# Attention and a mixture of experts in one kernel: a second block of tokens chosen from six batches' counts

## The chip, the cores and the metric

The kernel runs on one core of one Trainium2 chip. The metric is the device time of one execution, in microseconds; of the kernel before there are three, 904.43, 906.6 and 909.86 us, with a median of 906.6. Engines: TensorE (PE in rows), VectorE (DVE), ScalarE (ACT), GpSimd (POOL), and SyncE (SP), which here only issues DMAs.

## The reference

Eight batches of 448 tokens, 12 heads of 64. Attention with a soft cap on the scores, then for each token the one expert of eight with the largest logit, a two-layer network, scaled by the probability of that expert:

```python
def _attn_ref(q, k, v, cap):                      # (8, 12, 448, 64)
    scores = np.matmul(q, k.transpose(0, 1, 3, 2)) / np.sqrt(64)
    scores = cap * np.tanh(scores / cap)
    attn = softmax(scores)
    return np.matmul(attn, v)
...
def _moe_ref(x, w_gate, w1, w2):                  # (3584, 768), (768, 8), (8, 768, 1024), (8, 1024, 768)
    logits = x @ w_gate
    expert_idx = np.argmax(logits, axis=1)
    gate_w = softmax(logits)[np.arange(N), expert_idx]
    for e in range(8):
        xe = x[expert_idx == e]
        out[expert_idx == e] = gate_w * (np.maximum(xe @ w1[e], 0.0) @ w2[e])
```

## The kernel before

**Attention** runs in 48 steps, one for each pair of heads (six to a batch), and the steps overlap by hand. In step n TensorE makes the scores of pair n (`scores`, two parts), ScalarE their tanh and exp, VectorE adds up the parts of the probabilities (`adds`, whose second half ends with an addition on GpSimd, line 285, up to step 45), and TensorE multiplies the probabilities of pair n - 1 with V (`pv`). A list of tasks (`at(step, when, ...)`, run by `do`) puts the other work between these parts: the sums of the probabilities and the logits of a batch on TensorE, then on VectorE, batch by batch, the reciprocals (`rec_v`, `rec_c`), the logits (`log_v`), the choice of an expert (`route_v`, `route_g`), the scaling (`scale`), and the place of each token in its expert's list (`place_v`). SyncE stores the finished rows to DRAM (`store`), GpSimd scatters the token numbers to a list in DRAM (`place_d`, four scatters a batch). `filler` holds generators of small VectorE instructions; each `fill()` in the code runs one of them.

**Loads of Q, K and V** come by SyncE for two pairs at a time (`load(g, part)`). Before, K is asked for at the start of each even step and Q and V at the start of the next; the buffers are those of two groups earlier, so the transfer waits for the scores that still read them, and what is behind it on SyncE's queue waits too.

**The experts** work on blocks of tokens of one expert: large ones of 448 and small ones of 256. In a block, `up(j, f)` makes the half chunk f of the hidden layer (18 matmuls) and `down(j, f)` adds its share to the output (18 more), f from 0 to 7. Weights and x are float32, split into a high part (a cast on ScalarE, `high`) and what is left of it (a subtraction on VectorE or, with `e=G`, on GpSimd, `low`); three products of such halves stand for one. So each chunk of weights costs a cast and a subtraction, and x costs, for each of six pieces, a transposition on VectorE (`trans_x`), a cast on ScalarE and a subtraction on VectorE (`split_x`). h is split likewise behind `up`: a relu on ScalarE and one instruction of VectorE.

Which tokens form a block is known from the counts of all eight batches, from which VectorE works out tables (`tables`, some 40 small instructions). One block, number -1, is chosen earlier, from the counts of the first four batches (`first_block`): the expert with most tokens, in groups of 56. Its weights are loaded by SyncE in 16 chunks (`load_w0`, 384 KB each), its x gathered by GpSimd in 14 pieces of 128 rows (`load_x`) during the last steps of attention. The other eight (`ORDER`: six large, two small) get weights and x by gathers of GpSimd with the tables' indices; weights are not loaded again where a block has the expert of the one before. If the tables find more blocks than these, a branch at the end runs them.

The stretch that the change touches most is written out by hand: steps 42 to 48, then block -1 (`up(-1, 0)` to `down(-1, 7)`), between whose chunks the last two batches are routed and the tables are made, and then the start of the next block. Instructions of an engine run in the order of this text.

Of the kernel before, what the change touches and what calls it, by code (L numbers as in the profile page):

```python
# [18 lines left out]
E = 8  # L19
# [11 lines left out]

LARGE = 448
SMALL = 256
GROUP = 56
B_FIRST = 4

NL = (T - B_FIRST * S // E + E * (LARGE - SMALL - 1)) // LARGE
NS = E

ORDER = [0, 1, 2, 3, 4, 5, NL, NL + 1]  # L40
# [84 lines left out]
def attention_moe(tc, qT, kT, vL, capd, wgL, w1a, w1b, w2a, w2b, cst, cmk, out):  # L125
# [6 lines left out]

    n_first = (B_FIRST + 1) * NP + 1

# [404 lines left out]
    f0 = {}  # L539
# [3 lines left out]
    def first_block():  # L543
        cnt = att.tile([128, E], F32, name="cnt0")
        V.tensor_tensor(out=cnt, in0=base, in1=cb0, op=ALU.subtract)
        mx = att.tile([128, 1], F32, name="mx0")
        V.tensor_reduce(out=mx, in_=cnt, axis=AX.X, op=ALU.max)

        th = att.tile([128, LARGE // GROUP], F32, name="th0")
# [3 lines left out]
        k = keep.tile([128, 3], F32, name="k56")  # L553
        V.tensor_reduce(out=k[:, 0:1], in_=th, axis=AX.X, op=ALU.add)
        for i, f in ((1, -float(GROUP)), (2, GROUP / LARGE)):
            V.tensor_scalar(out=k[:, i : i + 1], in0=k[:, 0:1], scalar1=f, scalar2=None, op0=ALU.mult)
        V.tensor_scalar(out=cnt, in0=cnt, scalar1=mx, scalar2=None, op0=ALU.subtract)
        em, oh = first_max(cnt, [128, E], keep, "fb")
        e0 = keep.tile([128, 1], F32, name="e0")
        V.tensor_scalar(out=e0, in0=em, scalar1=8.0, scalar2=None, op0=ALU.add)  # L560
        t = att.tile([128, 2], F32, name="t0")
        V.tensor_scalar(out=t[:, 0:1], in0=e0, scalar1=128.0, scalar2=pcol, op0=ALU.mult, op1=ALU.add)
        V.tensor_scalar(
            out=t[:, 1:2], in0=e0, scalar1=float(T // QB), scalar2=kcol(C_IN), op0=ALU.mult, op1=ALU.add
        )

# [3 lines left out]
        V.tensor_tensor(out=t[:, 1:2], in0=t[:, 1:2], in1=mx, op=ALU.add)  # L570
        ti = keep.tile([128, 2], I32, name="t0i")
        V.tensor_copy(out=ti, in_=t)
        row = nc.values_load(
            ti[0:1, 0:1],
# [5 lines left out]
        f0.update(e0=e0, oh=oh, ti=ti, row=row, less=k[:, 1:2], part=k[:, 2:3])  # L580
# [3 lines left out]
    def tables():  # L584

        def tl(shape, name, dt=F32):
# [8 lines left out]
        V.scalar_tensor_tensor(  # L595
            out=cnt, in0=f0["oh"], scalar=f0["less"], in1=cnt, op0=ALU.mult, op1=ALU.add
        )
        yield 1
# [34 lines left out]
        for i, s, w in parts:  # L633
# [44 lines left out]
        V.tensor_scalar(  # L678
            out=first, in0=ej, scalar1=f0["e0"], scalar2=f0["part"], op0=ALU.is_equal, op1=ALU.mult
        )  # L680
        yield 1
        V.tensor_tensor(out=pr, in0=pr, in1=first, op=ALU.add)
        yield 1
# [17 lines left out]
        V.tensor_copy(out=prev[:, 0:1], in_=f0["e0"])  # L701
# [69 lines left out]
    def load_w0(i):  # L771

        f, r, w = (i, w1r, w1L) if i < FC else (i - FC, w2r, w2L)
        c = f % 4 * DM
        nc.sync.dma_start(out=r[f // 4][:, f % 4, :], in_=w[f // 4][bass.ds(f0["row"], 128), c : c + DM])
# [32 lines left out]
    def load_ids(j):  # L808
# [5 lines left out]
        idx = f0["ti"][:, 1:2] if j < 0 else tab["lidx"][:, j : j + 1]  # L814
# [29 lines left out]
    def load_x(j, gs=None):  # L844
        xi = idt[j][0]
        rows = 4 * S * (B_FIRST if j < 0 else B)
        for g in gs or range(groups(j)):
            gather(xg[:, g, :], xd[0:rows, :], xi[:, g : g + 1], rows - 1)
# [26 lines left out]
    def up(j, f):  # L875
# [11 lines left out]
        hb = h0 if j < 0 and f < 3 else m["hb"]  # L887
# [4 lines left out]
    def down(j, f, cs=range(2)):  # L892
        hh, hl = hs[j, f]
        wh, wl = w2s[f]
        if f == 0 and cs[0] == 0:
            if j < 0:
# [29 lines left out]
    def evac(j, cs=range(2)):  # L926
        y = m["y"]
        if cs[0] == 0:
            ys[j] = ys0 if j < 0 else m["yo"].tile([128, QB * XW], F32, name="ys")
# [41 lines left out]
    for b in range(B):  # L971
# [20 lines left out]
        at(n + 5, 0, store, b, range(0, 2))  # L992
        at(n + 5, 1, place_v, b)
        at(n + 6, 0, store, b, range(2, 4))
# [4 lines left out]
    at(n_first, 1, first_block)  # L999
    for i in range(2 * FC):  # L1000
        at(n_first + 1 + i, 1, load_w0, i)

    at(n_first + 4, 1, load_ids, -1)
    at(n_first + 6, 1, make_idx, -1)

    g = 0
    for i in range(7):
# [346 lines left out]
```

## Time and profile before

| | us |
|---|---|
| median of three runs | 906.6 |
| the profiled execution | 905.34 |
| its span in the profile | 903.6 |
| TensorE busy, matmuls | 838.4 (93%) |
| VectorE busy | 548.7 (61%) |
| ScalarE busy | 483.9 (54%) |
| GpSimd busy | 466.0 (52%) |
| mean granted clock of TensorE | 0.977 |

Attention fills the first 380 us, the nine blocks of the experts the rest. The page names lines of the kernel: 248 and 260 are the scores, 249, 263, 266 and 268 tanh and exp, 277 and 285 the adds, 300 and 310 the product with V, 884 `up`, 908 and 916 `down`, 889 and 890 the split of h, 791 and 796 the split of weights, 858, 864 and 865 that of x, 750 the gathers, 527 the scatters of token numbers. A timeline row gives the start, the duration, the engine, the operation with the tiles that it writes and reads, how many instructions are merged into it, and in brackets how long the engine had been idle and what released it.

### The profile page before, as it was taken

The numbers are of one execution on the slowest core, as the hardware profiler recorded it, in microseconds if no ns is written. First come the engines' busy times: TensorE is split into PE (matmuls) and PEld (weight loads), VectorE is DVE, ScalarE is ACT, GpSimd is POOL, SyncE is SP. The second block draws the span as 40 slices with busy tenths as digits, with TensorE's granted clock in tenths as the row PEclk, the third lists the DMA queues.
The fourth block names the chain that finished last, engine by engine and source line by source line (L and its number), as shares of the span: only waits on it lengthen the run. The fifth ranks groups of instructions, "written<-read, shape, count | busy, mean of one in ns | idle before, by whom it ended". The sixth has DMA issues, their size and how long they took to land. (4 is left out here: it accounts for less than half of the span.)

```text
span 903.6 us, 12040 instructions
## 1 busy us (share of the span) xinstructions
PE 838.4 (93%) x4492; PEld 557.4 (62%) x4492; DVE 548.7 (61%) x885; ACT 483.9 (54%) x573; POOL 466.0 (52%) x382
## 2 busy tenths in 40 slices
PE   8999999999999996786999999999999999999893
PEld 3222322222223221265989989899999999999893
DVE  3559797979797965777373763744735537356520
ACT  7988889888978883632332532332423324234410
POOL 1423353434343645653718857577577575665600
PEclk9999999999999997998999999999999999999997
DMA  5231545454527572404455312453431124444100
GB/s 202 70 123 62 182 65 181 65 181 66 180 97 210 173 246 89 64 16 126 154 202 193 127 27 62 180 188 128 169 127 53 32 64 176 183 177 173 65 34 33
DMA packets 45155, 111.67 MB, mean 124 GB/s; under 512 B 8561, under 2 KB 27411, under 8 KB 42016
## 3 DMA queue, kind: packets, MB, share of 16 engines
q1 hardware_dynamic: 28384, 50.72, 19.6%
q0 software_dynamic: 16416, 59.87, 18.8%
q8 instruction: 37, 0.61, 0.3%
q14 instruction: 30, 0.25, 0.1%
q10 hardware_dynamic: 288, 0.23, 0.1%
HBM read 101.40 MB, written 22.36 MB: 137 GB/s over the span
## 5 line engine op out<-in xcount | busy, mean ns | idle before, releaser
L285 POOL TENSOR_TENSOR p<-p,pr 64x896 f32<-64x896 f32 x46 | 103.4, 2248 | 206.7 <-DVE p L277 150.3
L889 ACT ACTIVATE hb<-ph 128x448 fp32r<-128x448 f32 (+1 forms) x69 | 34.9, 508 | 296.7 <-PE ph L884 208.1
L890 DVE SCALAR_TENSOR_TENSOR hb<-ph,hb 128x448 fp32r<-128x448 f32 (+1 forms) x69 | 39.3, 574 | 202.6 <-ACT hb L889 202.5
L249 ACT ACTIVATE pt<-sp,qsc 128x896 f32<-128x896 f32 x144 | 138.7, 997 | 35.0 <-PE sp L248 34.9
L750 POOL DMA_INDIRECT xg<-xd,xi x114 | 134.5, 1180 | 37.9 <-issue 30.4
L248 PE MATMUL sp<-qr,kr 64*128 64x448 f32 x576 | 136.9, 580 | 11.1 <-ACT pt L249 10.9
L266 ACT ACTIVATE pt<-pt,capt 128x1792 f32<-128x1792 f32 (+1 forms) x96 | 134.9, 1406 | 2.3
L310 PE MATMUL po<-pt,vr 128*64 128x448 f32 x576 | 132.4, 568 | 0.0
L760 POOL DMA_INDIRECT out<-ys,xi x98 | 107.9, 1101 | 29.2 <-issue 27.0
L248 PEld LDWEIGHTS sp<-qr,kr 64*128 64x128 f32 x576 | 47.8, 187 | 98.7 <-ACT pt L249 43.7
L277 DVE TENSOR_TENSOR p<-pt 128x896 f32<-128x896 f32 x48 | 58.3, 1214 | 48.9 <-ACT pt L266 48.9
L310 PEld LDWEIGHTS po<-pt,vr 128*64 128x64 f32 x576 | 33.5, 138 | 76.4 <-issue 74.4
L277 DVE TENSOR_TENSOR p<-p,pt 128x896 f32<-128x896 f32 x48 | 53.8, 1121 | 9.6 <-ACT pt L266 9.5
L864 ACT CAST xh<-xt 128x448 fp32r<-128x448 f32 (+1 forms) x54 | 27.2, 532 | 42.6 <-DVE xt L858 42.6
L527 POOL DMA_INDIRECT ids<-tok,slots x32 | 38.4, 1200 | 10.9 <-issue 6.3
L319 DVE COPY ot<-po 128x448 f32<-128x448 f32 x48 | 29.7, 619 | 20.7 <-PE po L310 20.5
L300 PE MATMUL po<-pr,vr 64*64 64x448 f32 x192 | 25.0, 565 | 15.1 <-ACT pr L268 14.2
L750 POOL DMA_INDIRECT w1r<-in_w1b,widx x8 | 11.1, 1382 | 46.1 <-DVE w17l L796 45.5
L858 DVE STREAM_TRANSPOSE xt<-xg 128x448 f32<-128x448 f32 (+1 forms) x54 | 30.3, 585 | 7.3 <-DMA xg<-xd,xi 6.4
L865 DVE TENSOR_TENSOR xl<-xt,xh 128x448 fp32r<-128x448 f32 (+1 forms) x54 | 28.8, 559 | 2.6 <-ACT xh L864 2.5
L934 DVE STREAM_TRANSPOSE ys<-y 128x448 f32<-128x448 f32 x36 | 19.8, 612 | 12.8 <-DMA out<-ys,xi 7.3
L300 PEld LDWEIGHTS po<-pr,vr 64*64 64x64 f32 x192 | 5.3, 131 | 33.2 <-ACT pr L268 31.5
(410 smaller groups left out, 1970.6 us busy)
## 6 DMA issues: line engine op xcount, KB each, us to landing
vr<-in_vL SPq DMA_DIRECT2D x24, 448.0 KB, 6.2
kr<-in_kT SPq DMA_DIRECT2D x23, 448.0 KB, 3.7
qr<-in_qT SPq DMA_DIRECT2D x23, 448.0 KB, 6.0
xd<-yt SPq DMA_DIRECT2D x20, 336.0 KB, 6.8
xd<-w2r SPq DMA_DIRECT2D x12, 336.0 KB, 5.8
xg<-xd,xi POOLq DMA_INDIRECT x114, 3.1
out<-ys,xi POOLq DMA_INDIRECT x98, 2.4
w1r<-in_w1a SPq DMA_DIRECT2D x4, 384.0 KB, 6.2
```

Of the source, the lines that this page charges most:

```text
L248: PE.matmul(sp[:, j, 0:S], kr[r, i, c], qr[r, i, :], start=True, stop=True)
L249: A.activation(out=pt[:, 2 * g : 2 * g + 2, :], in_=sp[:, 0:2, 0:S], func=AF.Tanh, scale=qsc)
L266: A.activation(out=pt[:, lo:hi, :], in_=pt[:, lo:hi, :], func=AF.Exp, scale=capt)
L277: V.tensor_tensor(out=p4, in0=pt[:, 0:2] if half == 0 else p4, in1=pt[:, 2 * half + 2 : 2 * half + 4], op=ALU.add)
L285: e.tensor_tensor(out=p4[r], in0=p4[r], in1=rests[n // 2][r], op=ALU.add)
L300: PE.matmul(pvs[n + i][64 * j : 64 * j + 64, 0:S], vr[r, 12 + j, :], rests[n // 2][r, j], start=True, stop=False,)
L310: PE.matmul(po[64 * j : 64 * j + 64, 0:S], vr[:, n % 2 * 6 + 3 * j + t, :], pt[:, 2 * t + j], start=False, stop=t == 2,)
L527: i = G.indirect_dma_start(out=ids, out_offset=bass.IndirectOffsetOnAxis(ap=slots[0:p, c : c + 1].bitcast(U32), axis=0), in_=tok[0:p, c : ...
L750: G.indirect_dma_start(out=dst, out_offset=None, in_=src, in_offset=bass.IndirectOffsetOnAxis(ap=idx.bitcast(U32), axis=0), bounds_check=b ...
L760: i = G.indirect_dma_start(out=dst, out_offset=bass.IndirectOffsetOnAxis(ap=idx.bitcast(U32), axis=0), in_=src, in_offset=None, bounds_che ...
L889: A.activation(out=hh, in_=ph, func=AF.Relu)
L890: V.scalar_tensor_tensor(out=hl, in0=ph, scalar=0.0, in1=hh, op0=ALU.max, op1=ALU.subtract)
```

## The change

A second early block, number -2, is chosen by the same function from the counts of six batches, less what block -1 takes. `ORDER` has one large block fewer. Its choice is handed out as small instructions by `fill()` from the end of step 42 on, the rest of it at the end of step 46; its 14 gathers of x are issued in steps 47 and 48; its weights come by SyncE, each of 16 chunks right behind the split that frees its place (`split`). Everything of block -1 moves one to two steps ahead: its choice from step 31 to 30, its weight chunks from steps 32 to 47 to 31 to 46, its gathers from steps 37 to 43 to 35 to 41, the split of its x from steps 44 to 48 to 42 to 46. The scatters of `place_d` move from 7 and 9 steps behind a batch's end to 6 and 7 (batch 4: from step 44 to 36 and 37; batch 5: from 45 and 46 to 42 and 43); `store` moves to the end of its step. The loads of Q, K and V for two pairs are all issued at the end of the scores of an odd step. In block -1 all weights from w12 on are subtracted on VectorE (w12 to w15 were on GpSimd), the tables are handed out in portions of four to seven between the chunks, and neither weights nor x of the next block depend on them any more.

```diff
-B_FIRST = 4
+B_FIRST = (4, 6)
-ORDER = [0, 1, 2, 3, 4, 5, NL, NL + 1]
+ORDER = [0, 1, 2, 3, 4, NL, NL + 1]
...
-    n_first = (B_FIRST + 1) * NP + 1
+    n_first = (B_FIRST[0] + 1) * NP
...
-    def first_block():
+    def first_block(i):
...
+        for f in early_blocks:
+            V.scalar_tensor_tensor(out=cnt, in0=f["oh"], scalar=f["less"], in1=cnt, op0=ALU.mult, op1=ALU.add)
+            yield 1
...
+    def first_row(i):
+        f = early_blocks[i]
+        f["row"] = nc.values_load(
+            f["ti"][0:1, 0:1],
+            engines=[mybir.EngineType.SP],
...
-    def load_w0(i):
+    def load_w0(j, i):
         f, r, w = (i, w1r, w1L) if i < FC else (i - FC, w2r, w2L)
         c = f % 4 * DM
+        nc.sync.dma_start(out=r[f // 4][:, f % 4, :], in_=w[f // 4][bass.ds(early_blocks[-1 - j]["row"], 128), c : c + DM])
...
-        at(n + 5, 0, store, b, range(0, 2))
+        at(n + 5, 2, store, b, range(0, 2))
...
-        if b < B_FIRST:
+        if b < B - 2:
             for q in range(4):
-                at(n + 7 + 2 * (q // 2), 1, place_d, b, q)
+                at(n + 6 + q // 2, 1, place_d, b, q)
...
+    at(n_first, 1, lambda: [None for _ in first_block(0)])
+    at(n_first, 2, first_row, 0)
+    at(n_first + 3, 1, load_ids, -1)
+    at(n_first + 4, 1, make_idx, -1)
+    for i, w in enumerate((2, 1, 1, 3, 3, 3, 1)):
+        at(n_first + 5 + i, 2, load_x, -1, range(g, g + w))
+        g += w
+    for n, k in ((6, 0), (6, 1), (5, 2), (4, 3), (4, 4), (2, 5)):
+        at(n_pairs - n, 2, trans_x, -1, k)
+        at(n_pairs - n, 2, split_x, -1, k, V)
     at(n_pairs - 2, 2, split_w1, 0, G)
+    second = first_block(1)
+    at(n_pairs - 6, 2, filler.append, second)
+    at(n_pairs - 2, 1, lambda: [None for _ in second])
+    at(n_pairs - 2, 1, load_ids, -2)
+    at(n_pairs - 1, 1, first_row, 1)
+    at(n_pairs - 1, 1, make_idx, -2)
+    at(n_pairs - 1, 2, load_x, -2, range(0, 4))
     at(n_pairs, 0, split_w1, 1, G)
+    at(n_pairs, 1, load_x, -2, range(4, QB))
...
-        if n // 2 * 2 + 4 < n_pairs:
-            load(n // 2 + 2, n % 2)
...
             scores(n, 1)
+            if n % 2 and n + 3 < n_pairs:
+                for part in range(2):
+                    load(n // 2 + 2, part)
...
+    def split(i, f):
+        (split_w1, split_w2)[i - 1](f)
+        load_w0(-2, FC * (i - 1) + f)
+    for f in range(2):
+        load_w0(-2, f)
     rec_v(b)
-    split_w1(2, G)
-    split_w1(3, G)
+    split(1, 2)
     up(-1, 1)
     rec_p(b)
+    split(1, 3)
     rec_c(b)
     log_v(b)
-    high(1, 4)
     up(-1, 2)
-    low(1, 4, G)
+    split(1, 4)
     log_p(b)
     route_v(b)
     route_s(b)
+    up(-1, 3)
+    place_p(b)
+    split(1, 5)
+    place_v(b)
+    for i in (b - 1, b):
+        for q in range(4):
+            place_d(i, q)
+    up(-1, 4)
+    split(2, 0)
     turn(n_pairs - 2)
     turn(n_pairs - 1)
+    up(-1, 5)
+    split(2, 1)
     route_g(b)
     scale(b, 0, V)
+    down(-1, 0)
+    split(2, 2)
     scale(b, 1, V)
     store(b)
-    load_ids(0)
-    load_w(0, 0, (0,))
-    make_idx(0)
-    load_x(0)
+    filler.append(tables())
+    fill(6)
     down(-1, 1)
+    split(2, 3)
+    fill(6)
+    split(1, 6)
     down(-1, 2)
...
-    blocks = [-1] + ORDER
+    blocks = [-1, -2] + ORDER
```

## Rows read from the trace of the kernel before

**Rows 1.** Part 2 of the page: busy tenths of TensorE and its granted clock.

```profile
PE   8999999999999996786999999999999999999893
...
PEclk9999999999999997998999999999999999999997
```

**Rows 2.** Stretches: length; busy us (count) of PE, PEld, DVE, ACT, POOL; PEclk; DMA; GB/s.

```profile
345.00:360.00 15.00, 8.49 (x26) 2.83 (x26) 9.78 (x20) 7.01 (x9) 6.72 (x6) 0.66 0.04 8
405.00:420.00 15.00, 9.53 (x41) 8.08 (x40) 13.40 (x52) 5.54 (x9) 5.48 (x5) 0.81 0.17 34
```

**Rows 3.** Timeline of TensorE: start us, us, engine, line, operation, count [idle before <- releaser].

```profile
278.53 1.77 PE L248 MATMUL sp<-qr,kr 64*128 64x448 f32 x8
...
337.32 1.77 PE L248 MATMUL sp<-qr,kr 64*128 64x448 f32 x8
...
380.31 0.47 PE L884 MATMUL ph<-xh,w10h 128*128 128x448 f32 x1
...
386.38 0.47 PE L884 MATMUL ph<-xh,w10h 128*128 128x448 f32 x1 [3.33 <-ACT xh L864]
...
417.45 0.74 PE L908 MATMUL z<-yt,w20l 128*128 128x448 f32 x1 [4.12 <-DVE w20l L796]
...
435.38 0.37 PE L884 MATMUL ph<-xh,w16h 128*128 128x448 f32 x1
...
457.24 0.37 PE L884 MATMUL ph<-xh,w10h 128*128 128x448 f32 x1
```

**Rows 4.** Timeline of VectorE and ScalarE around x of the first block.

```profile
347.16 0.65 DVE L858 STREAM_TRANSPOSE xt<-xg 128x448 f32<-128x448 f32 x1 [6.44 <-DMA xg<-xd,xi]
...
347.84 0.56 ACT L864 CAST xh<-xt 128x448 fp32r<-128x448 f32 x1 [8.49 <-DVE xt L858]
...
348.44 0.63 DVE L865 TENSOR_TENSOR xl<-xt,xh 128x448 fp32r<-128x448 f32 x1 [0.63 <-ACT xh L864]
...
359.09 0.56 ACT L864 CAST xh<-xt 128x448 fp32r<-128x448 f32 x1 [5.09 <-DVE xt L858]
...
370.80 0.56 ACT L864 CAST xh<-xt 128x448 fp32r<-128x448 f32 x1 [3.69 <-DVE xt L858]
...
379.57 0.56 ACT L864 CAST xh<-xt 128x448 fp32r<-128x448 f32 x1 [1.88 <-DVE xt L858]
```

**Rows 5.** Timeline of VectorE, TensorE and GpSimd, adds and gathers of steps 38 to 45.

```profile
294.55 1.07 DVE L277 TENSOR_TENSOR p<-p,pt 128x896 f32<-128x896 f32 x1
...
312.58 0.96 PE L341 MATMUL ps_s<-p,cs 128*32 128x448 f32 x8
...
316.65 1.76 DVE L277 TENSOR_TENSOR p<-p,pt 128x896 f32<-128x896 f32 x1 [0.59 <-ACT pt L266]
...
317.61 1.69 POOL L750 DMA_INDIRECT xg<-xd,xi  x1 [0.15 <-issue]
...
323.68 1.09 DVE L277 TENSOR_TENSOR p<-p,pt 128x896 f32<-128x896 f32 x1 [0.52 <-ACT pt L266]
...
325.89 2.10 POOL L285 TENSOR_TENSOR p<-p,pr 64x896 f32<-64x896 f32 x1 [6.59 <-issue]
...
363.72 2.88 POOL L285 TENSOR_TENSOR p<-p,pr 64x896 f32<-64x896 f32 x1 [10.86 <-DMA ids<-tok,slots]
```

**Rows 6.** Part 5 of the page: the gathers of x, all of them.

```profile
L750 POOL DMA_INDIRECT xg<-xd,xi x114 | 134.5, 1180 | 37.9 <-issue 30.4
```

**Rows 7.** The line of the gathers, 290 to 350 us: issue to landing.

```profile
DMA to landing us min/median/max: 2.8/5.0/8.1
```

**Rows 8.** Timeline of VectorE in the first block: tables, then a subtraction.

```profile
405.74 0.16 DVE L592 TENSOR_TENSOR cnt<-base,kc 128x8 f32<-128x8 f32 x1
...
420.25 0.16 DVE L734 TENSOR_TENSOR mor<-more 128x1 int32<-128x1 f32 x1
...
423.63 0.95 DVE L796 TENSOR_TENSOR w21l<-w2r,w21h 128x768 fp32r<-128x768 f32 x1
```

**Rows 9.** Waits of SyncE's queue: total us, times, longest.

```profile
SPq L176 <- PE sp L248: 250.3, 22, 14.0
```

More of the change, by code (lines that the diff above doesn't have):

```diff
@@ L569, in first_block @@
         )
[L570 to L574, printed above, removed]
+        yield 1
+        V.tensor_tensor(out=ts[:, 1:2], in0=ts[:, 1:2], in1=mx, op=ALU.add)
+        yield 1
+        ti = tl(keep, [128, 2], "ti", I32)
+        V.tensor_copy(out=ti, in_=ts)
+        yield 1
+        early_blocks.append(dict(e0=e0, oh=oh, ti=ti, less=k[:, 1:2], part=k[:, 2:3]))
+    def first_row(i):
+        f = early_blocks[i]
+        f["row"] = nc.values_load(
+            f["ti"][0:1, 0:1],
             engines=[mybir.EngineType.SP],
@@ L593, in tables @@
         yield 1
[L595 to L598, printed above, removed]
+        for f in early_blocks:
+            V.scalar_tensor_tensor(
+                out=cnt, in0=f["oh"], scalar=f["less"], in1=cnt, op0=ALU.mult, op1=ALU.add
+            )
+            yield 1
         t1 = tl([128, E, 8], "t1")
@@ L677, in tables @@
         first = tl([128, n], "first")
[L678 to L683, printed above, removed]
+        for f in early_blocks:
+            V.tensor_scalar(
+                out=first, in0=ej, scalar1=f["e0"], scalar2=f["part"], op0=ALU.is_equal, op1=ALU.mult
+            )
+            yield 1
+            V.tensor_tensor(out=pr, in0=pr, in1=first, op=ALU.add)
+            yield 1
         li = tl([128, n], "li")
@@ L700, in tables @@
         yield 1
-        V.tensor_copy(out=prev[:, 0:1], in_=f0["e0"])
+        V.tensor_copy(out=prev[:, 0:1], in_=early_blocks[-1]["e0"])
         yield 1
@@ L1077, in attention_moe @@
     assert not tasks
-    split_w1(2, G)
-    split_w1(3, G)
+    split(1, 2)
     up(-1, 1)
     rec_p(b)
+    split(1, 3)
     rec_c(b)
     log_v(b)
-    for q in range(4):
-        place_d(b - 1, q)
-    high(1, 4)
     up(-1, 2)
-    low(1, 4, G)
+    split(1, 4)
     log_p(b)
@@ L1097, in attention_moe @@
     w2s[3] = chunk(hw2, "w23")
-    up(-1, 3)
-    low(1, 5, G)
-    place_p(b)
-    place_v(b)
-    high(1, 6)
-    filler.append(tables())
-    fill(8)
-    up(-1, 4)
+    up(-1, 5)
+    split(2, 1)
     route_g(b)
-    low(1, 6)
-    high(1, 7)
-    for q in range(4):
-        place_d(b, q)
     scale(b, 0, V)
-    up(-1, 5)
-    fill(6)
-    low(1, 7)
+    down(-1, 0)
+    split(2, 2)
     scale(b, 1, V)
     store(b)
-    split_w2(0)
-    fill(100)
-    load_ids(0)
-    load_w(0, 0, (0,))
-    make_idx(0)
-    load_x(0)
-    load_w(0, 1, (0,))
-    load_ids(1)
-    down(-1, 0)
-    split_w2(1)
-    split_w2(2)
-    split_w2(3)
-    load_w(0, 0, (1,))
+    filler.append(tables())
+    fill(6)
     down(-1, 1)
+    split(2, 3)
+    fill(6)
+    split(1, 6)
     down(-1, 2)
```

105 lines of the change are left out of this document (56 added, 49 removed).

## The prediction

> **What bounds the kernel now.** The page's slices come first: TensorE is busy in nine tenths and more of nearly every slice, and the one weak place is around slices 15 to 18, about 345 to 425 us, where the granted clock falls too [rows 1]. The table of stretches says how weak: of 345 to 360 us TensorE works 8.5 us, at a mean clock of 0.66, and of 405 to 420 us 9.5 us at 0.81 [rows 2]. Elsewhere nothing is to be had: the change neither adds nor removes a matmul. So the whole question is what the end of attention and the first block of tokens, which run into each other here, cost before and after.
>
> The timeline of TensorE gives both prices [rows 3]. Pair step 37 begins at 278.53 and step 45 at 337.32: 7.35 us a step while all is well. From 337.32 three steps (22.1 us) and the rest of the last pair (its PV matmuls and its logits, some 3.5 us) should end at 362.9; the first block starts at 380.31. **17.4 us are lost at the end of attention.** The block runs from 380.31 to 457.24, 76.9 us. Its sixteen half chunks cost 3.64 us each where nothing waits (six from 435.38 to 457.24), 58.3 us in all, and the last batch's small matmuls between them some 2.8 us, an estimate from eight such in 0.96 us [rows 5]. **15.8 us are lost in the first block**; the longest pieces are 3.3 us for x and 4.1 us for w20l [rows 3].
>
> Why, by the rows of ScalarE and VectorE [rows 4]. Each step from 44 to 47 transposes a piece of x on VectorE and casts it on ScalarE. VectorE stands 6.4 us for the gathers of x; the cast, in order on ScalarE, makes that 8.5 us without a tanh; the next casts hold ScalarE for 5.1, 3.7 and 1.9 us, since VectorE reaches its transposition only behind the batch's routing and the add. ScalarE has little slack, so TensorE starves. In the block, w20l comes at 417.45 because VectorE runs the tables (405.74 to 420.25) and routing ahead of it [rows 8].
>
> **The change, part by part.** *Work of TensorE:* with the reference's inputs the largest expert has 1343 tokens after four batches and 895 are left, so the second early block is full; five large and two small blocks remain. Nine blocks run before and after. The second block always loads its weights, some 6 MB more than a skipped load; after 457 us DMA has room, so I price that at nothing (if it had none, a block would wait a few us).
>
> *The first block's stage.* Removed: the wait for x (3.3 us and the slow matmuls behind it), since the last piece of x is split in step 46 (before, step 48); the subtractions of w12 to w15 on GpSimd; and the tables ahead of w20l, which go out six at a time between chunks. Added on VectorE: those four subtractions at 0.95 us [rows 8]. I lay VectorE's queue beside TensorE, counted from the block's start, with chunks of 3.64 us, small instructions at 0.2 and transpositions at 0.65 us [rows 4, 8]. Sums and logits of the last batch stand behind chunk 0, so `rec_v` runs from 5.3 to 7.6; w12l ends at 8.5; chunk 1 ends near 10, its h_low at 11; w13l at 12; `rec_c` and `log_v` at 15.3. TensorE wants `log_p` at 14 and stands 1.4 us. `route_v` and w14l end at 19, in time for `place_p` at 19.5; w15l, `place_v` and the next h_low bring w20l to about 25.5, and `down` 0 wants it at 27. Every later subtraction has over 1 us to spare. On GpSimd w11l now stands behind four gathers of the second block's x; they wait for the index made at the end of step 47 and take 4 × 1.5 us [rows 6], so w11l ends near 7 where chunk 1 wants it at 6.5: 0.7 us. With 0.5 us of small change I leave 2.6 us of the 15.8: **a gain of 13.2 us**. The second block's own start is as block 0's was: w20 is split behind its chunk 1 in both.
>
> *SyncE.* 250 us are spent there waiting to load K for the next pair [rows 9]. The new place issues all three loads behind the scores that free the buffers. What lay behind that wait (stores, weight chunks) may go earlier, but the loads themselves leave at the same scores, so the traffic comes in the same bursts; its price is nothing. The wait on the row of the second block stands ahead of two stores of batch 6 and costs nothing as long as the choice of the block is made by step 46: it has 18 small instructions, handed out over some 20 openings between the adds of steps 43 to 46.
>
> *The end of attention.* The pieces of x move from steps 44 to 48 to steps 42 (two), 43, 44 (two) and 46. Per step I take ScalarE's time without a tanh or an exp: 2.0 us till the transposition is done where no routing is ahead (8.49 less 6.44, and the 1.88 of step 47), 5.1 us behind routing, 3.7 in step 46, 0.6 for a cast, and 2.0 for a second piece in the same step (hand-over 0.63, subtraction 0.63, transposition, cast) [rows 4]. Before: 9.1 + 5.7 + 5.1 + 3.3 = 23.2 us, with the casts of w10 and w11 (an estimate of 0.8 each, by the subtraction's 0.95 [rows 8]), of which 17.4 showed; slack swallowed 5.8. After: 4.6 + X in step 42, 5.7 in step 43 (behind `rec_v` and the handed-out choice), 4.6 in step 44, 5.1 in step 46, 0.8 in step 47: 20.8 + X, with the same slack 15.0 + X. X is the wait for the gathers, and the whole forecast hangs on it.
>
> *X.* The gathers move from steps 37 to 43 to steps 35 to 41, their use from step 44 to 42: the distance stays, but three steps in a row now hold three gathers and one more follows, where before ones and threes alternated, and four scatters of ids have moved into steps 36 and 37. What GpSimd does with that shows in [rows 5]: an add of an odd step starts only when the gathers or scatters ahead of it have landed. The gather of step 40 was issued at 317.61, the add of step 41 was ready by 318.4 and started at 325.89; another add stood 10.9 us for scatters. I chain that with an add at 2.1 us, a gather at 1.5 (1.18 and 0.3 to issue) and the median landing of 5.0 us [rows 6, 7]. The add of step 38 (VectorE ready at 295.6) ends at 301.8, 4 us late already, since the add of step 37 waited for scatters; three gathers to 306.3; the last lands at 309.8; add 39 to 311.9, gathers to 316.4; add 40 to 318.5, gathers to 323.0; the last lands at 326.5; add 41 to 328.6; its single gather, issued at 328.9, lands 2.8 to 5.0 later, about 332.8. VectorE wants it behind the add of step 42, at 324.8. **X is 8 us**, against 6.4 before. With landings of 2.8 us and gathers of 1.2 X is 0; with 8.1 and 1.7 it is 17. I take the median since bursts of SyncE's traffic continue as they were.
>
> The Trainium skill ("DMA: Bandwidth & Descriptors", section "Anatomy of one DMA — SWDGE (gpsimd) path") gives about 2.0 us plus bytes over 436 GB/s for a DMA issued by GpSimd, an estimate of 2.2 us for a gather of 98 KB, by which X would be 0; the trace has 2.8 to 8.1 us [rows 7] and decides; what would follow from that figure is the first rival.
>
> So attention's end costs 23 instead of 17.4 us: **a loss of 5.6 us**. GpSimd's other DMAs have slack: sums read an add two steps later.
>
> **Sum.** The profiled execution took 905.34 us (span 903.6), 1.3 below the median of 906.6. 905.3 − 13.2 + 5.6 = 897.7, say **898 us**.
>
> **Rivals.** *The stall goes away* (X = 0): gathers land in about 3 us because stores and chunks no longer pile up behind SyncE's wait. For it: landings of 2.8 us do occur [rows 7]; against it: the loads come in the same bursts. Attention then costs 15.0: 905.3 − 13.2 − 2.4 = 890.
>
> *A new wait in the first block*: each half chunk hangs on ScalarE's cast and VectorE's subtraction right ahead of it, eight hand-overs with 1 to 2 us to spare. If VectorE runs 6 us later than in my list, the gain is 7: 904. Against it: GpSimd does no arithmetic there any more but w11l.
>
> *GpSimd's backlog grows* (the slower side): with landings of 8.1 us the add of step 39 ends at 316, while TensorE wants it for the sums at 312.6 [rows 5], and X is 17. Attention then costs 32 us and 4 for the sums: 905.3 − 13.2 + 18.6 = 911, and scatters landing as late as the 10.9 us row make it 913. It decides where add 41 starts over 12 us behind its inputs; for it speaks the add that already stood 7 us.
>
> *The change doesn't do what it says*: an empty second block or one more block at the end would cost 59 us or so; the counts speak against it.
>
> **How the numbers follow.** Forecast 0.57 (893 to 903, X from 3 to 13), stall gone 0.20 (888 to 892), new wait 0.12 (902 to 907), backlog 0.08 (911 to 916), rest 0.03. About 0.5%, 4.5 us, is what a measurement can tell from no change: faster means below 902. From the forecast 0.50 falls there and 0.07 within; so faster 0.70, same 0.21 (with the new wait and the rest), slower 0.09. The range of 888 to 908 leaves out a part of the fast case and all of the backlog.
>
> **What would show it.** Right: block one spans some 64 us without a wait for w20l; VectorE waits for xg in step 42, 4 to 12 us, with ScalarE behind it and the clock down; GpSimd's add of step 41 starts far behind its inputs. Wrong: no wait for xg (then 890), TensorE waiting for a weight's low half or h in the block (then 904), or for the adds in the sums (then 911).

## The result, and the profile after

| | before | after |
|---|---|---|
| median of 14 runs, us | 907.36 (904.43 to 910.61) | 911.70 (909.42 to 915.26) |
| ratio, 95% interval | | 1.0053 (1.0035 to 1.0071) |
| profiled execution, us | 905.34 | 909.42 |
| its span | 903.6 | 907.6 |
| block -1 starts | 380.31 [rows 3] | 399.07 |
| block -2 (before: block 0) starts | 457.24 [rows 3] | 462.55 |
| length of block -1 | 76.9 | 63.5 |

The change makes the kernel slower by half a per cent; 898 us had been forecast. Here and below, medians and ratios leave out the executions in a second, slower state of the chip, such as one of 1075 us among e4's four. The table already holds the outline. The first block of tokens gained what it was to gain, 13.4 us. The end of attention lost 18.8 us where 5.6 had been forecast. From block -2 on, after runs some 5 us behind before and ends 4 us behind. By the busy times of TensorE from 270 us to the start of block -1 (95.2 of 110.3 us before, 98.9 of 129.1 after), 15.0 of the 18.8 us are idle time; in the other 3.7 its matmuls run at a mean granted clock of 0.87 and not 0.94. In block -1 (66.1 of 76.9 us before, 62.1 of 63.5 after) 9.4 us of the gain are idle time that is gone, and 4.1 come from a mean clock of 1.00 and not 0.93.

The page of after, part 2 (40 slices of 22.7 us: TensorE, its granted clock, share of the DMA engines, what they moved):

```profile
PE   8999999999999676889999999999999999999893
...
PEclk9999999999999788899999999999999999999997
DMA  5231667666778674146924472543441124544100
GB/s 185 85 122 62 137 113 145 126 120 145 143 183 123 105 256 108 42 118 122 205 88 146 169 303 67 188 182 103 171 149 54 36 57 174 185 178 174 66 33 32
```

The weak place of [rows 1] is now wider and begins earlier, in slices 13 to 17, from 295 us on. The DMA line is as telling: in slices 4 to 13 the DMA engines are busy 6 to 8 tenths at 105 to 183 GB/s, where slice 23 moves 303 GB/s in 7 tenths; they are occupied and move little.

Waits of TensorE in after between 280 and 480 us (engine, tile, line <- releaser: us in all, times, longest), and then those of block -1 alone, from 399 to 463 us:

```profile
PE ps_s L343 <- POOL p L287: 12.8, 2, 8.3
PE sp L250 <- ACT pt L251: 12.7, 4, 6.1
PE ps_l L431 <- DVE lr L426: 3.2, 2, 2.0
...
```

```profile
PE ps_l L431 <- DVE lr L426: 1.2, 1, 1.2
PE ph L921 <- POOL w11l L833: 0.2, 1, 0.2
```

Timeline of TensorE in after, the sums of the probabilities and the starts of the two early blocks:

```profile
303.22 1.71 PE L343 MATMUL ps_s<-p,cs 128*32 128x448 f32 x4 [8.34 <-POOL p L287]
...
325.06 1.71 PE L343 MATMUL ps_s<-p,cs 128*32 128x448 f32 x4 [4.45 <-POOL p L287]
...
399.07 0.47 PE L921 MATMUL ph<-xh,w10h 128*128 128x448 f32 x1
...
462.55 0.36 PE L921 MATMUL ph<-xh,w10h 128*128 128x448 f32 x1
```

The first line of the waits is new: 12.8 us for the sums, in two pieces, which wait for GpSimd's adds (line 287; line 285 before). In before the sums of that stretch start without a wait, as those at 312.58 us in [rows 5] do. In block -1 itself only 1.4 us of waiting are left: the 4.1 us for w20l of [rows 3] are gone.

Why the add was late stands on GpSimd's and SyncE's queues of after:

```profile
277.00 2.09 POOL L287 TENSOR_TENSOR p<-p,pr 64x896 f32<-64x896 f32 x1 [1.45 <-DVE p L279]
279.25 1.03 POOL L529 DMA_INDIRECT ids<-tok,slots  x1 [0.17 <-issue]
280.59 1.72 POOL L529 DMA_INDIRECT ids<-tok,slots  x1 [0.31 <-issue]
282.62 1.05 POOL L787 DMA_INDIRECT xg<-xd,xi  x1 [0.30 <-issue]
301.10 2.06 POOL L287 TENSOR_TENSOR p<-p,pr 64x896 f32<-64x896 f32 x1 [17.43 <-DMA xg<-xd,xi]
```

```profile
281.94 0.36 SPq L178 DMA_DIRECT2D kr<-in_kT  x1
282.35 0.43 SPq L180 DMA_DIRECT2D qr<-in_qT  x1
282.82 0.43 SPq L182 DMA_DIRECT2D vr<-in_vL  x1
283.45 1.79 SPq L812 DMA_DIRECT2D w1r<-in_w1b  x2
```

GpSimd had stood idle for 17.4 us when the gather landed and the add of step 37 could start at 301.10. In front of that add are two scatters of token ids (line 529), a gather, and, from SyncE at the same moment, K, Q and V of the next pairs and two chunks of weights. What the DMA engines did in 270 to 300 us (40 slices of 0.75 us; then issues with KB each and median us to landing):

```profile
DMA  9968999999920000099009984647699991326999
GB/s 354 258 140 329 366 371 419 371 359 391 354 83 23 0 1 0 0 86 53 0 14 115 29 33 19 38 29 38 57 24 33 53 43 5 29 33 163 382 408 418
...
kr<-in_kT SPq DMA_DIRECT2D x1, 448.0 KB, 16.4
```

From 286.5 to 295 us they are busy for four to nine tenths of the time and move 19 to 57 GB/s; K takes 16.4 us to land. By the pages, the loads of K take 3.7 us in the median in before, 7.2 in after, and 3.5 in c3 below, a version with a remedy (in this order):

```profile
kr<-in_kT SPq DMA_DIRECT2D x23, 448.0 KB, 3.7
```

```profile
kr<-in_kT SPq DMA_DIRECT2D x23, 448.0 KB, 7.2
```

```profile
kr<-in_kT SPq DMA_DIRECT2D x23, 448.0 KB, 3.5
```

The records of single packets in the trace of after agree: a packet of 3584 bytes, the size of K's, takes 140 ns in the median, and the longest of the 28 begun between 282 and 284 us took 8.7 us.

### The profile page after: what moved, and what is told of

The parts are those of the page before. It is cut to its first block, busy times and chain, and to the rows that moved or that the text cites. A ratio compares the mean times of both kernels' runs of the same rounds, so it can differ in the third digit from the quotient of the medians.

```text
span 907.6 us, 12126 instructions
## 1 busy us (share of the span) xinstructions
PE 841.0 (93%) x4492; PEld 557.0 (61%) x4492; DVE 543.7 (60%) x913; ACT 484.9 (53%) x573; POOL 450.8 (50%) x374
## 5 line engine op out<-in xcount | busy, mean ns | idle before, releaser
L287 POOL TENSOR_TENSOR p<-p,pr 64x896 f32<-64x896 f32 x46 | 105.8, 2299 | 219.8 <-DVE p L279 91.4
L250 PE MATMUL sp<-qr,kr 64*128 64x448 f32 x576 | 140.6, 593 | 13.2 <-ACT pt L251 13.1
L787 POOL DMA_INDIRECT xg<-xd,xi x114 | 131.0, 1149 | 39.7 <-issue 32.3
L279 DVE TENSOR_TENSOR p<-pt 128x896 f32<-128x896 f32 x48 | 54.2, 1129 | 47.4 <-ACT pt L268 47.2
L312 PEld LDWEIGHTS po<-pt,vr 128*64 128x64 f32 x576 | 33.4, 138 | 76.9 <-issue 74.2
L529 POOL DMA_INDIRECT ids<-tok,slots x32 | 35.5, 1108 | 8.8 <-issue 5.2
L343 PE MATMUL ps_s<-p,cs 128*32 128x448 f32 x192 | 27.3, 568 | 12.8 <-POOL p L287 12.8
## 6 DMA issues: line engine op xcount, KB each, us to landing
w2r<-in_w2a SPq DMA_DIRECT2D x8, 384.0 KB, 13.2
```

Source lines behind the costliest of these rows:

```text
L250: PE.matmul(sp[:, j, 0:S], kr[r, i, c], qr[r, i, :], start=True, stop=True)
L279: V.tensor_tensor(out=p4, in0=pt[:, 0:2] if half == 0 else p4, in1=pt[:, 2 * half + 2 : 2 * half + 4], op=ALU.add)
L287: e.tensor_tensor(out=p4[r], in0=p4[r], in1=rests[n // 2][r], op=ALU.add)
L312: PE.matmul(po[64 * j : 64 * j + 64, 0:S], vr[:, n % 2 * 6 + 3 * j + t, :], pt[:, 2 * t + j], start=False, stop=t == 2,)
L529: i = G.indirect_dma_start(out=ids, out_offset=bass.IndirectOffsetOnAxis(ap=slots[0:p, c : c + 1].bitcast(U32), axis=0), in_=tok[0:p, c : ...
L787: G.indirect_dma_start(out=dst, out_offset=None, in_=src, in_offset=bass.IndirectOffsetOnAxis(ap=idx.bitcast(U32), axis=0), bounds_check=b ...
```

## What was tried

The theories, as the expectations name them. **A**: the scatters of token ids, which the change moved next to the loads, slow down every transfer issued behind them, so gathers land late, so GpSimd's adds are late for the sums. **B**: GpSimd's own backlog of three gathers a step does it (the prediction's third rival). **C**: the loads of K, Q and V in one burst do it.

The runs were made in five sets, each with the kernel before beside it. In the first three sets before took 12 to 15 us longer (919 to 922 us), and the versions of after that were also timed outside them 16 to 19 (c1, e9, e10); in the traces of b1, e9 and e10 the eighth block takes 48 to 50 us instead of 35. Why is open, and kernels are compared within a set or by their ratio to before. The traces of these three sets hold next to no landing times, so what the expectations say of landings is read from sets 4 and 5.

| set | kernel | us, median | ratio to before, 95% interval |
|---|---|---|---|
| 1 | before | 919.46 | |
| | e1 scatters 7 and 9 steps behind a batch | 938.07 | 1.0175 (1.0119 to 1.0230) |
| | e2 loads at the old places | 933.16 | 1.0154 (1.0097 to 1.0210) |
| | e3 gathers and pieces of x at the old steps | 944.28 | 1.0249 (1.0199 to 1.0299) |
| | e4 before, with the new scatters alone | 961.21 | 1.0465 (1.0380 to 1.0549) |
| 2 | before | 921.82 | |
| | c1 after | 930.81 | 1.0117 (1.0073 to 1.0161) |
| | e5 late scatters | 914.23 | 0.9911 (0.9862 to 0.9960) |
| | e6 late scatters, wide scatters in their place | 918.06 | 0.9950 (0.9906 to 0.9994) |
| | e7 late scatters, old loads | 918.42 | 0.9975 (0.9947 to 1.0003) |
| 3 | before | 922.35 | |
| | e8 ids in rows of 64 bytes | 915.13 | 0.9937 (0.9912 to 0.9962) |
| | e9 ids 64 bytes apart | 914.60 | 0.9920 (0.9890 to 0.9949) |
| | e10 late scatters and rows of 64 bytes | 914.56 | 0.9918 (0.9887 to 0.9948) |
| | b1 before, with rows of 64 bytes | 923.19 | 1.0005 (0.9978 to 1.0033) |
| 4 | before | 907.58 | |
| | c2 after | 914.71 | 1.0072 (1.0045 to 1.0099) |
| | e11 as e10, pieces of x a step later | 896.66 | 0.9885 (0.9858 to 0.9911) |
| | e12 as e11, end scatters later | 896.35 | 0.9883 (0.9856 to 0.9910) |
| 5 | before | 906.02 | |
| | c3 as e9 | 896.83 | 0.9900 (0.9856 to 0.9944) |
| | c4 as e10 | 896.21 | 0.9879 (0.9834 to 0.9924) |
| | e13 as e11, last piece in step 46 | 896.90 | 0.9884 (0.9842 to 0.9927) |

**Undoing one part each (e1, e2, e3).**

```diff
 e1
-                at(n + 6 + q // 2, 1, place_d, b, q)
+                at(n + 7 + 2 * (q // 2), 1, place_d, b, q)
 e2
+        if n // 2 * 2 + 4 < n_pairs:
+            load(n // 2 + 2, n % 2)
...
-            if n % 2 and n + 3 < n_pairs:
-                for part in range(2):
-                    load(n // 2 + 2, part)
 e3
-    for i, w in enumerate((2, 1, 1, 3, 3, 3, 1)):
+    for i, w in enumerate((3, 1, 3, 1, 3, 1, 2), 2):
-    for n, k in ((6, 0), (6, 1), (5, 2), (4, 3), (4, 4), (2, 5)):
+    for n, k in ((4, 0), (3, 1), (2, 2), (1, 3), (0, 4), (0, 5)):
...
-    at(n_pairs - 1, 2, load_x, -2, range(0, 4))
...
-    at(n_pairs, 1, load_x, -2, range(4, QB))
+    at(n_pairs, 2, load_x, -2)
```

> The changed kernel with one part undone: each batch's four scatters of token ids leave again two by two at the ends of two odd steps (n+7 and n+9), and not at the end of an even step and of the odd one behind it (n+6 and n+7). Theory A (the scatters of 4-byte elements, issued just ahead of the K, Q and V loads, make these crawl, so gathers land late, so GpSimd's adds come late for the sums): the loads between 270 and 330 us land in 4 to 8 us instead of 12 to 20, TensorE's wait for the sums falls from 12.8 us to under 2, and the time is 895 to 900 us. Theory B (GpSimd's backlog of three gathers a step is the cause by itself): the sums' wait stays over 6 us, 904 to 911. Theory C (all three loads of a pair in one burst are the cause): the landings stay at 12 us and more, 908 to 913.

> The changed kernel with the loads of a pair back at the starts of two steps (K in the even one, Q and V in the odd one), the rest as changed. Theory C: the landings fall to 4 to 8 us, the sums' wait goes, 895 to 900 us. Theory A: the scatters still stand ahead of K, Q and V, which wait for the same scores; the wait for the sums stays at 8 us or more, and the time within 3 us of the changed kernel's 911.7. Theory B: the same as A.

> The changed kernel with the gathers of the first block's x back in steps 37 to 43 (3, 1, 3, 1, 3, 1, 2 a step), its pieces back in steps 44 to 48, and the gathers of the second block's x behind the last piece; the scatters of ids stay at n+6 and n+7. Theory B: no wait for the sums over 2 us; attention's end costs 17 us again as in the kernel before, the first block is 3 to 5 us longer for x: 900 to 905 us. Theory A: K, Q and V of step 37 still land in 12 us or more, and the adds behind the scatters are late, but there are fewer gathers behind them: TensorE waits 4 to 10 us for the sums or later for x, 907 to 915.

None of them brought the time back; after itself, timed in the next set, has 1.0117. C falls with e2: with the old loads the sums still wait 14.0 us. B falls with e3, whose add of step 37 has only scatters ahead of it and no gather, and waits all the same (the sums wait 15.8 us); GpSimd's timeline of e3:

```profile
279.36 1.02 POOL L529 DMA_INDIRECT ids<-tok,slots  x1 [0.17 <-POOL p L287]
280.69 1.73 POOL L529 DMA_INDIRECT ids<-tok,slots  x1 [0.31 <-issue]
298.73 2.06 POOL L287 TENSOR_TENSOR p<-p,pr 64x896 f32<-64x896 f32 x1 [16.31 <-DMA ids<-tok,slots]
```

A, as I had put it, falls with e1. There the scatters leave 7 and 9 steps behind every batch's end. For batches 4 and 5 that undoes only a part of the change, since theirs left from step 44 on before: batch 4's first pair, now in step 37, is followed by four gathers, and by K, Q and V 5 us later, and the add of step 39 waits 13.4 us; the sums' wait is 12.9 us, as in after. K, Q and V are issued at 310.30 us; GpSimd's timeline of e1:

```profile
303.55 1.57 POOL L529 DMA_INDIRECT ids<-tok,slots  x1 [0.28 <-POOL p L287]
305.43 1.44 POOL L529 DMA_INDIRECT ids<-tok,slots  x1 [0.31 <-issue]
307.17 1.48 POOL L787 DMA_INDIRECT xg<-xd,xi  x1 [0.30 <-DVE lt L412]
...
314.27 1.00 POOL L787 DMA_INDIRECT xg<-xd,xi  x1 [0.30 <-issue]
328.62 2.06 POOL L287 TENSOR_TENSOR p<-p,pr 64x896 f32<-64x896 f32 x1 [13.36 <-DMA xg<-xd,xi]
```

So it is not only the place just ahead of the loads that counts: whatever follows a pair of scatters closely is slow, gathers too (here the last is issued 9 us behind the pair). (e1 has a second burden: the ids of block -1 are gathered some 12 us later than in after, behind the scatters of step 33.) Before, a gap of 9 us stood between the first pair of batch 3 and the next K, by GpSimd's and SyncE's timelines; the scatters land in 8.5 us in the median (issues of 240 to 270 us), while next to nothing else moves, and K lands in 3.5:

```profile
245.88 0.99 POOL L527 DMA_INDIRECT ids<-tok,slots  x1 [0.28 <-POOL p L285]
247.18 0.97 POOL L527 DMA_INDIRECT ids<-tok,slots  x1 [0.30 <-issue]
```

```profile
256.13 0.33 SPq L176 DMA_DIRECT2D kr<-in_kT  x1
```

```profile
DMA  4899997982000002000000479999899300000000
...
kr<-in_kT SPq DMA_DIRECT2D x1, 448.0 KB, 3.5
...
ids<-tok,slots POOLq DMA_INDIRECT x4, 8.5
```

**One part alone (e4).** The kernel before, with the scatters at the new steps:

```diff
-        if b < B_FIRST:
+        if b < B - 2:
             for q in range(4):
-                at(n + 7 + 2 * (q // 2), 1, place_d, b, q)
+                at(n + 6 + q // 2, 1, place_d, b, q)
...
-    for b in (B_FIRST, B_FIRST + 1):
-        for q in range(4):
-            at(n_first + 13 + (b - B_FIRST) + (q > 1) * (b > B_FIRST), 1, place_d, b, q)
```

> The kernel before with one part of the change alone: the scatters of ids of batches 0 to 5 at n+6 and n+7. Theory A: landings of K, Q and V rise from 3.5 to 6 us to 8 us and more in each batch; in the quiet batches TensorE pays nothing; in steps 37 to 40, where gathers follow, GpSimd's adds come late for the sums by 2 to 10 us: 907 to 917 against 906.6. Theories B and C: within 2 us of the kernel before, and the landings as they were.

Slower by 4.7%, where A had given 1.2% at most and the others nothing. From its page, the group of the sums with the wait in front of it:

```profile
L341 PE MATMUL ps_s<-p,cs 128*32 128x448 f32 x192 | 32.1, 599 | 25.4 <-POOL p L285 25.4
```

Nothing else of the change is in this kernel, so the scatters' place alone is enough. With before's later gathers (steps 37 to 43) batch 5's scatters meet gathers too: an add behind them waits 11.5 us at 373 us, where in after the gathers are over. The 25.4 us are not all that is lost; the rest isn't broken down here.

**The scatters out of the way (c1, e5, e6, e7).** In e5 the scatters of batches 4 and 5 leave in steps 43 and 44, behind the last loads; e7 has the old loads besides.

```diff
-                at(n + 6 + q // 2, 1, place_d, b, q)
+                at(n + 6 + q // 2 if b < 4 else 39 + b, 1, place_d, b, q)
```

> The changed kernel as it is, timed beside the others of this set, since the kernel before took 907 us in one set of runs and 919 in another. All theories: 1.003 to 1.015 of the kernel before, a wait of 10 us or more for the sums in steps 39 and 41, loads between 270 and 330 us landing in 12 us and more.

> The changed kernel with one thing different: the scatters of ids of batches 4 and 5 leave at the ends of steps 43 and 44 (four each), behind the last K, Q and V loads and the last gather of x, and not in steps 36, 37, 42 and 43. Theory A (what is issued while scatters of 4-byte elements are in flight, crawls; loads and gathers then keep GpSimd's adds from the sums): no wait for the sums over 1.5 us, add 37 starts within 8 us of its inputs, loads between 270 and 330 us land in 4 to 8 us; 13 us less than the changed kernel, 0.985 to 0.99 of the kernel before; if the gathers of x land faster too, VectorE's wait for them falls from 6.4 us to under 3 and it is 0.98. Theory B (backlog of three gathers a step): the wait for the sums stays over 5 us, within 4 us of the changed kernel. Theory C (the bursts of loads): the same as B.

> The version with the late scatters, and the loads of a pair back at the starts of two steps (K in the even, Q and V in the odd). Theory A: the placement of the loads is worth under 2 us either way, so the same time as with the late scatters alone. Theory C: 5 us or more faster than the version with late scatters alone.

e5 is 16.6 us faster than after in the same set and faster than before: A, in the wider form. It missed two expectations: 7.2 us of waits for the sums are left before 280 us, where the scatters of batches 0 to 3 still meet loads (0.9 us behind it), and VectorE's wait for x is 7.4 us, not under 3. e7 gives no support to C either: it is 4 us slower than e5, where A had the same time within 2 us; the intervals overlap.

e6 puts into steps 36 and 37 of e5 scatters of as many rows, each 512 bytes:

```diff
+        G.indirect_dma_start(
+            out=probe,
+            out_offset=bass.IndirectOffsetOnAxis(ap=slots[0:p, c : c + 1].bitcast(U32), axis=0),
+            in_=cs[0:p, 0:128],
...
+    for q in range(4):
+        at(36 + q // 2, 1, probe_d, 4, q)
```

> The version with the late scatters, and in steps 36 and 37, where the changed kernel had the scatters of batch 4's ids, two scatters each of as many rows at the same row numbers, but of 512 bytes a row (constants, to a memory that nothing reads). If it is the element of 4 bytes that makes them slow, these land in 3 to 5 us and cost under 3 us; if any scatter of 128 scattered rows does it, add 37 starts over 10 us late, the sums wait 8 us or more and the gain of the late scatters is gone.

```profile
292.12 1.03 POOL L546 DMA_INDIRECT probe<-cs,slots  x1 [0.17 <-issue]
294.70 0.99 POOL L546 DMA_INDIRECT probe<-cs,slots  x1 [1.54 <-DMA probe<-cs,slots]
296.00 1.04 POOL L801 DMA_INDIRECT xg<-xd,xi  x1 [0.30 <-issue]
301.98 2.08 POOL L287 TENSOR_TENSOR p<-p,pr 64x896 f32<-64x896 f32 x1 [4.94 <-DMA xg<-xd,xi]
```

The second of the pair waits for the first and starts 1.5 us after that was issued: 128 rows of 512 bytes land within 2.6 us of their start, and the add waits 4.9 us, not 17.4. The cost is 3.8 us by the medians, against an expected 3 at most; the intervals overlap, and these scatters wait for one another, which those of the ids don't.

**What makes them slow (e8, e9, e10, b1).** In e8 each id has 64 bytes of its own and all are written; in e9 only 4 of them. The list of ids is filled and gathered with the same spacing. e10 has rows of 64 bytes and e5's late scatters, b1 is before with rows of 64 bytes.

```diff
 e8
-    ids = dpool.tile([(E + 1) * T, 1], I32, name="ids")
+    ids = dpool.tile([(E + 1) * T, 16], I32, name="ids")
...
-            in_=tok[0:p, c : c + 1],
+            in_=tok[0:p, c : c + 16],
 e9
+    ids = dpool.tile([(E + 1) * T * 16, 1], I32, name="ids")
...
-        V.tensor_copy(out=slots[:, b * 4 : b * 4 + 4], in_=slot)
+        V.tensor_scalar(out=slots[:, b * 4 : b * 4 + 4], in0=slot, scalar1=16.0, scalar2=None, op0=ALU.mult)
```

> The changed kernel with its own schedule of scatters, but each id stands in a row of 64 bytes of its own (16 integers, of which the first is read), so a scatter writes 128 rows of 64 bytes and the gather of ids reads 16 times as much. Two causes for the slow scatters: S (several writes of 4 bytes go to the same line of memory, 14 to 16 ids of an expert side by side, and are served one after the other) and P (any write smaller than some hundreds of bytes is slow). By S the scatters land in 3 to 5 us, the loads behind them in 4 to 8 us, the waits for the sums fall under 4 us and the time is 0.985 to 0.992 of the kernel before; by P it stays at 1.008 to 1.015.

> The changed kernel with ids 64 bytes apart as in the run with rows of 64 bytes, but only the 4 bytes of each are written. By S (crowding in the same line is what is slow) this is as fast as rows of 64 bytes, 0.985 to 0.992 of the kernel before; by P (the size of each write) the scatters still land in 8 us and more, the loads behind them in 12 us, and it is 1.008 to 1.015.

> Both remedies: rows of 64 bytes, and the scatters of batches 4 and 5 behind the last loads. If the slow scatters were all that went wrong, nothing is left of the waits for the sums, also in the batches before 270 us, and what is left is what the prediction had: 0.98 to 0.99 of the kernel before; if the backlog of gathers matters too, the waits for the sums stay at 5 us.

> The kernel before with ids in rows of 64 bytes and nothing else changed. If its own scatters cost time on this chip too (919 to 922 us there against 907 elsewhere), this gives it back: 0.985 to 0.99 of the kernel before. If not, 0.998 to 1.003 (the larger fill of the table at the start costs under 2 us), and the gain of the changed kernel with such rows is the change's own.

All three versions of after are at 0.992 to 0.994, and e9 is no slower than e8; the sums wait 2.7 us in e8, 1.6 in e9 and 1.5 in e10, against 15.0 in c1. So neither the 4 bytes nor the number of writes is slow, but writes of 4 bytes side by side: S. e10 misses its 0.98 to 0.99 by a little. Before gains nothing by it (1.0005): its scatters slow loads too, as the last paragraph on the prediction shows, but in before no sum waits for an add.

**The prediction's own sum (c2, c3, c4, e11, e12, e13).** The last two sets time the remedies where before takes 906 to 908 us. e11 takes the pieces of x a step later, e13 all but the last; e12 moves the eight scatters of the last batches behind `down(-1, 2)`.

```diff
 e11
-    for n, k in ((6, 0), (6, 1), (5, 2), (4, 3), (4, 4), (2, 5)):
+    for n, k in ((5, 0), (5, 1), (4, 2), (3, 3), (3, 4), (1, 5)):
 e13
+    for n, k in ((5, 0), (5, 1), (4, 2), (3, 3), (3, 4), (2, 5)):
 e12
-    for i in (b - 1, b):
-        for q in range(4):
-            place_d(i, q)
     up(-1, 4)
...
     down(-1, 2)
+    for i in (b - 1, b):
+        for q in range(4):
+            place_d(i, q)
```

> The changed kernel as it is, once more, beside the versions below. If the slow scatters are the loss: 1.005 to 1.015 of the kernel before. If the chip of the set made the difference: 0.99 to 0.997.

> The changed kernel with ids 64 bytes apart and 4 bytes written of each, nothing else, once more. If the prediction's other steps hold, 898 to 902 us where the kernel before takes 907 (0.988 to 0.994), with attention's end 5 to 7 us later than in the kernel before and the first block 13 to 14 us shorter.

> Rows of 64 bytes and the late scatters of batches 4 and 5, once more. If the scatters of ids cost nothing any more, the same as with ids 64 bytes apart alone, within 2 us; if they still hold GpSimd's adds back, 3 us or more faster.

> Rows of 64 bytes, late scatters of batches 4 and 5, and the pieces of x taken one step later (43, 43, 44, 45, 45 and 47, not 42, 42, 43, 44, 44 and 46). If the prediction's term for the end of attention holds (8 us of waiting for the gathers of x cost 5.6 us there), the wait for x falls under 2 us, the last scores come 5 us or more earlier than the 378.7 us of the run without this edit, and the time is 0.983 to 0.988 of the kernel before. If VectorE's routing and the casts of ScalarE are what costs the time there and not the gathers, or if the last piece now comes late for the block, it stays at 0.990 to 0.995.

> As with the pieces of x one step later, but the last piece stays in step 46 (43, 43, 44, 45, 45, 46). If the wait of the first block for the last piece (its first chunk ran beside the cast at 382 us) is what made that block 68 us, it falls to 64 or 65 and the time is 2 to 4 us under that of the pieces one step later (896.7 where the kernel before took 907.8); if step 46 is then the one that holds ScalarE, the last scores come 2 to 4 us later and nothing is gained.

> As the run with the pieces later, and the eight scatters of ids of batches 6 and 7, which leave ahead of chunk 4 of the first block, moved behind the third half chunk of its second matrix. If they hold ScalarE (its relu of chunk 4 waits 10 us, TensorE 5 to 7 us for w20), the first block falls from 66 to 73 us to about 63, 4 us or more less than without this edit. If ScalarE stands there for another reason, the same time as without it, or up to 2 us more, since the ids of block 0 come later.

c3 is the changed kernel without the crowding and nothing else: 896.83 us, where 898 had been forecast for the change and 898 to 902 for this run (its ratio lies in the expected range). GpSimd's timeline of c3 has the same scatters and the same gather within 3 us of the times of after; but where GpSimd then stands 17.4 us for the gather in after, it stands 5.2 here and VectorE releases it. Below it transfers issued from 270 to 330 us; in c2, the changed kernel in the set before, the same lines have 17.4 and 12.4 us:

```profile
282.10 1.03 POOL L532 DMA_INDIRECT ids<-tok,slots  x1 [0.16 <-issue]
283.43 1.72 POOL L532 DMA_INDIRECT ids<-tok,slots  x1 [0.31 <-issue]
285.46 1.04 POOL L790 DMA_INDIRECT xg<-xd,xi  x1 [0.30 <-issue]
291.70 2.08 POOL L290 TENSOR_TENSOR p<-p,pr 64x896 f32<-64x896 f32 x1 [5.20 <-DVE p L282]
```

```profile
kr<-in_kT SPq DMA_DIRECT2D x3, 448.0 KB, 3.4
...
ids<-tok,slots POOLq DMA_INDIRECT x4, 2.4
```

Its block -1 starts at 385.68 us and block -2 at 448.52: attention's end costs 5.4 us more than before, and the block is 62.8 us long. c4 equals it; so, the crowding gone, the place of the scatters is worth nothing that these runs can tell.

The pieces of x a step later (e11, e13) bring no time that these runs can tell either, against my expectation for e11. ScalarE's waits between 325 and 386 us, c4 first, then e13, show why for e13:

```profile
ACT xh L904 <- DVE xt L898: 21.6, 6, 9.2
```

```profile
ACT xh L904 <- DVE xt L898: 19.5, 6, 7.3
```

In c4 VectorE stood 8.3 us for x (6.4 in after); in e13 it does not wait for x at all, and yet ScalarE waits almost as long for the transposed pieces, now behind the routing on VectorE. Block -1 starts at 385.3 us in c4 and 384.5 in e13.

e11 is another case, since its last piece goes to step 47. VectorE doesn't wait for x, and attention does end earlier, nearly as expected: the last scores start at 374.7 us and block -1 at 379.81, 5.5 us before c4's (380.31 in before). But the block is then 68.3 us long (62.9 in c4). TensorE's timeline of e11, the starts of the two early blocks:

```profile
379.81 0.47 PE L924 MATMUL ph<-xh,w10h 128*128 128x448 f32 x1
...
448.06 0.37 PE L924 MATMUL ph<-xh,w10h 128*128 128x448 f32 x1
```

From 385 to 391 us TensorE works 3.4 of 6 us, with 2.0 us of waiting for w11l, and from 391 to 397 at a mean granted clock of 0.78 where c4 has 1.00. By 395 us both runs are level (`rec_p` at 394.80 us in e11, 394.97 in c4), and block -2 starts at 448.06 and 448.16. So an earlier end of attention is lost again at the start of the block. e13's last scores start 3.3 us later than e11's, as its expectation had it for the case that step 46 holds ScalarE.

e12 could not answer its question: the stall of ScalarE that it was to test, seen in some runs of sets 1 to 3 (TensorE waits 7.1 us for w20 in e10), is not there in set 4, with or without the edit. What that stall is stays open.

## Why the prediction was wrong

**Block -1**: 13.2 us forecast, 13.4 gained, a length of 63.5 where some 64 was named. The list of VectorE's queue beside the chunks held: of its two priced waits, 1.4 us for `log_p` and 0.7 for w11l, 1.2 and 0.2 are there, and nothing else waits (waits of block -1, above).

**The end of attention**: 5.6 us forecast, 18.8 measured. This is the failed term, and two steps of it failed together. One is the landing time: the chain for X took the median of 5.0 us "since bursts of SyncE's traffic continue as they were", with 8.1 as the bad end; with scatters ahead, adds stood 17.4 and 10.0 us for gathers. The loads' own new place is not to blame (e2, e7). The other is the treatment of the moved scatters: I counted their landing as a delay of one add and gave nothing for what they do to transfers beside them. And "sums read an add two steps later" was the cover that I named for GpSimd's lateness; it was used up, and TensorE waited 12.8 us beyond it. In c3, where the same scatters are not crowded, the end of attention costs 5.4 us.

**The third rival**, the backlog, had the right place (adds late for the sums, 911 us) with a chance of 0.08, and priced late scatters at 2 us more, but it did not have the right cause: c3 has the same backlog of three gathers a step, its sums wait 3.0 us, and it takes 897.

**The rest of the forecast** came out once the one cause was away: in c3 attention's end costs 5.4 us (5.6 forecast) and the block gains 14.1 (13.2). But the way to the 5.6 was only partly right, and that it agrees is in part luck: 3.0 us of c3's are a wait for the sums that the forecast did not have. "The whole forecast hangs on X" is wrong: X was 6.4 us in after and 9.5 in c3, and taking it away altogether (e13) moved the block's start by 0.8 us against c4, where the sum of the prediction would have it move by 8. ScalarE's waits behind VectorE's routing come up as X goes away; the first rival (890 us) was not to be had. Nor are the two terms of the sum independent: e11's attention ends 5.5 us earlier than c4's, and its block is 5.4 us longer.

**What the trace of before could have told**: [rows 5] has an add that stood 10.9 us for scatters of 128 ids each, half a kilobyte, longer than the gathers of 98 KB in [rows 7]. I read it as a delay of GpSimd alone. The price to the transfers beside it could be read there too, from the landing of each K. Three times K is issued 4.7 to 4.9 us behind the second scatter of a pair (at 118.67, 163.23 and 208.07 us), and lands in 7.7, 7.9 and 7.9 us; 5.7 us behind, in 5.0 to 5.7; 9 us behind, or with no scatter ahead, in 3.4 to 3.8. Issues of 163 to 164 us in before:

```profile
kr<-in_kT SPq DMA_DIRECT2D x1, 448.0 KB, 7.9
```

## What to carry to other kernels

Where a step that issues DMAs is moved, look at what will be in flight beside it, and not only at who waits for it: a transfer that is harmless in an idle gap can hold up what is issued close behind it. A small scattered write with a long landing is a warning, and spacing its targets is a cheap trial (here 2% between c1 and e9, by their ratios). A wait that a forecast hangs on should be taken away alone before its price is believed: what comes second may stand right behind it. And an earlier end of one stage counts only where the next stage can use it (e11).

## What the hardware showed

Four-byte writes to neighbouring places of DRAM are slow, and slow down others. A scatter of 128 ids lands in 8.5 us in the median with little else in flight (before), and in 12.4 with loads and gathers behind it (c2); with the ids 64 bytes apart the median is 2.4 us (c3). K's load lands in 17.4 us behind the former and 3.4 behind the latter. That it is the sharing of a piece of memory by several writes is the reading that fits e8 and e9; the runs don't show what the memory does, nor from which spacing on it is fast.

The Trainium skill ("DMA: Bandwidth & Descriptors", section "Specifications") says that below 512 bytes the DMA engine does a read-modify-write. If that had a price by size alone, e9, whose writes have 4 bytes, would have stayed slow, and it did not. The Trainium skill (the same title, section "Back-pressure in remote DMA") says, of transfers between cores, that stalled writes stall the other queues of their DMA engine too. K's loads on SyncE's queue, which take 16.4 us to land behind GpSimd's scatters, look alike within one core; that the cause is the same, no run here shows.
